# Attention and a bilinear GLU side by side on one core: other durations, leads and pauses in the planner that writes the order of work

## The chip, the cores and the metric

The kernel runs on one core of a Trainium2 chip. The metric is the device time of one execution in microseconds (us), the median of several runs. Before the change it is 2714.88 us (three runs, 2710.84 to 2721.91).

## The reference

What has to be computed, with S = 2048 rows, D = 576 columns, H = 32 heads of Dh = 18 and F = 4608 (the file writes the same with lambdas and einsum):

```python
xn  = layernorm(x)
# A: attention
q, k, v = heads(xn @ wqkv)
p   = softmax(q @ k.T * Dh ** -0.5)
s   = heads_joined(p @ v) @ wo
# B: bilinear GLU
h   = (xn @ w_gate) * (xn @ w_up)
g   = silu(h @ w_down)
out = x + s * g
```

All is float32. The kernel splits most operands into a high and a low part and multiplies three combinations of them, so one product of the reference is several matmuls here.

## The kernel before, in words

**Three stages.** A prologue normalises x, transposes it, makes q, k and v and spills q and k (`sqk`), v (`sv`) and the split columns of x (`sx`) to DRAM. The main stage computes attention and GLU together. The end stage multiplies the heads by `wo`, by the gate, and adds x.

**The main stage** has two streams of GLU work and two kinds of scores, and they share TensorE (PE) by rows of the array. Half 0 (rows 0 to 63) computes the up projection, half 1 (rows 64 to 127) the gate projection; matmuls of the two halves run at the same time if they stand next to each other in PE's queue. The GLU work comes in 72 units: 4 chunks of 512 rows of x by 18 pairs of 128 columns of F. In each unit both halves do two projections `n` of 27 matmuls with 512 columns (`gu_op`, L654), then the down projection of the unit before, 4 times 12 matmuls with 288 columns in each half (`down_op`, L682). `up_end` (L659) copies the up result on ACT; `gate_end` multiplies (L666, DVE), asks for the weights of projection n+2 (`g_get`, L183, DMA `wgu<-swg`), splits the product on ACT and POOL (L669, L670) and swaps halves by DMA (`hs<-hs`). `down_end` adds into `acc` (L710, DVE), and the last one of a unit asks for the next down weights (`d_get`, L216, DMA `wd<-swd`). In the first chunk the weights come raw and are split in small pieces on ACT and POOL (`piece`, L191/L192 and L222/L223) and stored for the later chunks.

**Scores.** For each head, 64 matmuls of the first kind (`a_item`, L558, usually half 0) give scores from which DVE takes maxima (L560). After the 64th, `max_fold` and `max_rows` (L566, L573, L574, L576) prepare the row maxima and write them into q by DMA. Then 64 matmuls of the second kind (`b_item`, L591, usually half 1) give scores that ACT exponentiates (L593). Each kind has two PSUM banks (`pa`, `pb`), the rest shares four (`pg`): a matmul may start in a bank only when the engine that reads it is done. When four groups of exponentials are there, a "visit" (`pv_group`, L602) multiplies them by v; it uses all 128 rows of the array, so both halves stop for it.

**The planner.** No engine chooses at run time: each runs its queue in order, and a wait at the head of PE's queue holds both halves. The order is written while the program is built. `order()` (L997) keeps a clock for each half (`clk`), a time at which DVE and ACT are free (`free`), a time at which each bank is free (`banks`), and a queue of DMAs at 0.24 MB per us (`moved`). At each step it takes the half whose clock is behind and gives it a score or the next matmul of its stream: a score when its bank is free and its goal (`a_goal`, `b_goal`, a pace over the whole stage) has passed, or when the stream may not go. `can_go` (L960) holds a stream back until its weights and inputs are believed to have landed (`loaded`, `there`, `downed`), and holds a gate projection until half 0 is `FIRST` us ahead. `lean` shifts the goals so that half 0 tends to be `SKEW` us ahead. `small` (L910) puts in the small chores: pieces of weights, and a list `later` that makes silu of a finished chunk and, after the first chunk, splits `wo` in five parts: `wo_load` (DMA into `wop`), `wo_high` (ACT, L766), `wo_low` (POOL, L770). Between two chores of `later` it lets 6 us of its own clock pass, or what `PAUSES` says.

The lines that the durations stand in, before:

```python
banks["a"][slot] = engine("DVE", clk[r] + 0.45, 0.70) + 0.06     # L872
clk[r] += 0.229                                                  # L873
rows_done[h] = engine("DVE", clk[r] + 0.45, 0.60) + ROWS         # L878
free[eng] = max(free[eng], start) + length - 0.09                # L837
clk[0] = clk[1] = now + 0.40                                     # L956, after a visit
```

Of the kernel before, what the change touches and what calls it, by code (L numbers as in the profile page):

```python
# [40 lines left out]
def kernel(  # L41
# [13 lines left out]
    H = 32  # L55
    DH = D // H
    assert S == 2048 and D == 576 and F % 256 == 0
    NT = S // 128
# [74 lines left out]
    chores, later = [], []  # L133
# [20 lines left out]
    units = [(c, q) for c in range(NCH) for q in range(NF2)]  # L154
# [51 lines left out]
    def d_get(n):  # L206
        if n >= len(units) - 1:
            return
        p = columns_of(n)
        if n and n % NF2 == 0:  # L210
            dw[n] = dw[n - 1]
            ddone.add(n)
            return
        w = dw[n] = d_tile()
        if n >= NF2:
            nc.sync.dma_start(w.bitcast(FT), swd[p])  # L216
            ddone.add(n)
            return
        raw = draw.pop(n)

        def piece(k):
            nc.scalar.activation(w[:, k, :, 0, :], raw[:, k], AF.Copy)  # L222
            nc.gpsimd.tensor_tensor(w[:, k, :, 1, :], raw[:, k], w[:, k, :, 0, :].bitcast(FT), op=OP.subtract)  # L223

        def end():
            ddone.add(n)
            nc.sync.dma_start(swd[p], w.bitcast(FT))
            d_load(n + 1)

        chores.extend([(piece, (k,)) for k in range(2)] + [(end, ())])  # L230

    R = 3 * DH

# [306 lines left out]
    with ExitStack() as mid:  # L540
# [236 lines left out]
        def wo_fetch():  # L777
# [2 lines left out]
            nc.sync.dma_start(wos[0].bitcast(FT), swo[:, 0:8, :])  # L780
            nc.sync.dma_start(wos[1].bitcast(FT), swo[:, 8:10, :])

        def stream(r):

            for u in range(len(units) + 1):
                for n in (2 * u, 2 * u + 1):
                    if u == len(units):
                        break
                    c, q = units[u]
                    box = []  # L790
                    for k in range(len(TERMS)):
                        def work(n=n, k=k, box=box, c=c, q=q):
                            if k == 0:
                                box.append(gu_start(r, n))
                            gu_op(r, n, box[0], k)
                            if q == NF2 - 1 and n % 2 and k % 3 == 2 and c < NCH - 1:
                                x_block(c + 1, k // 3, (64 * r,))
                                there["x", c + 1, k // 3, r] = moved(clk[r] + 0.5, 0.262)
                            if k == len(TERMS) - 1:
                                (gate_end if r else up_end)(n, box[0])  # L800
                                if r and n == 2 * len(units) - 1:
                                    wo_fetch()
                        end = (("DVE", 0.70) if r else ("ACT", 0.60)) if k == len(TERMS) - 1 else None
                        yield 0.229, k == 0, work, end, ("g", n, k)
                for s in range(4):
                    if not u:
                        break
                    box = []
                    for k in range(len(DTERMS)):
                        def work(s=s, k=k, box=box, u=u - 1):  # L810
                            if k == 0:
                                box.append(down_start(r, u))
                            down_op(r, u, s, box[0], k)
                            if k == len(DTERMS) - 1:
                                down_end(r, u, s, box[0])
                        end = ("DVE", 0.46) if k == len(DTERMS) - 1 else None
                        yield 0.131, k == 0, work, end, ("d", u - 1, 12 * s + k)

# [1 line left out]
        N = 64  # L822
        TOTAL = H * N
        LEAD, MOST = 24, 40
        PACE, SKEW, PULL, FIRST, ROWS = 1.01, 5.2, 3.0, 5.0, 6.0
        slots, gone = [0, 0], [0.0, 0.0]
        clk, free = [0.0, 0.0], {"DVE": 0.0, "ACT": 0.0}
        banks = {"a": [0.0] * 2, "b": [0.0] * 2, "g": [0.0] * 4}
        turn = {"a": 0, "b": 0}

        def next_free(tag):
            if tag == "g":
                return min(banks["g"])
            return banks[tag][turn[tag] % len(banks[tag])]

        def engine(eng, start, length):
            free[eng] = max(free[eng], start) + length - 0.09  # L837
            return free[eng] + 0.09

        def moved(start, size):  # L840

# [3 lines left out]
        due, jobs, rows_done = [], [], {}  # L845
        there, queue = {}, [0.0]
        na = nb = 0
        part = len(units) * (2 * 27 * 0.229 + 4 * 12 * 0.131) + (TOTAL + N + LEAD) * 0.229
        span = part + H * NT * (0.858 + 0.05)
        QUICK, LAST = 0.75, 0.75  # L850
        pace = (PACE * span - QUICK * N - LAST * (N + LEAD)) / (TOTAL - N)

# [8 lines left out]
        def a_next(r=0):  # L861
            nonlocal na
            h, i = divmod(na, N)
            if i == 0 and 2 <= h + 1 < H:
                stacks.append((0, h + 1))
            if i == 48 and (0, h + 1) in stacks:
                stacks.remove((0, h + 1))
                load_stack(0, h + 1)
            a_item(h, i, r)
            slot = turn["a"] % 2  # L870
            turn["a"] += 1
            banks["a"][slot] = engine("DVE", clk[r] + 0.45, 0.70) + 0.06  # L872
            clk[r] += 0.229  # L873
            na += 1
            if i == N - 1:
                max_fold(h)
                max_rows(h)
                rows_done[h] = engine("DVE", clk[r] + 0.45, 0.60) + ROWS  # L878

        def b_ready(r=1):  # L880
            h = nb // N
# [2 lines left out]
        def b_next(r=1):  # L884
            nonlocal nb
            h, i = divmod(nb, N)
            if i == 0 and h < H - 1:
                stacks.append((64, h + 1))
            if i == 48 and (64, h + 1) in stacks:
                stacks.remove((64, h + 1))  # L890
                load_stack(64, h + 1)
            if i == 16 and h % 2 == 0 and h // 2 + 1 < H // 2:
                load_v(h // 2 + 1)
            b_item(h, i, r)
            slot = turn["b"] % 2
            turn["b"] += 1
            end = engine("ACT", clk[r] + 0.45, 0.60)
            banks["b"][slot] = end + 0.06
            clk[r] += 0.229
            nb += 1  # L900
            if i % 4 == 3:
                due.append((h, i // 4, end + 0.1))

        KINDS = {"piece": ("ACT", 0.55), "first": ("ACT", 0.70), "second": ("DVE", 0.45), "inverse": ("DVE", 1.06),
                 "wo_high": ("ACT", 0.70)}
        PAUSES = {"wo_low": 16.0, "last": 16.0}

        quiet = [0.0]

        def small(now):  # L910

            q = chores or later
            if q is later and now < quiet[0]:
                return
            if q:
                eng, length = KINDS.get(q[0][0].__name__, ("POOL", 0.0))
                if eng == "POOL" or free[eng] <= now + 0.1 + (0.15 * (now - quiet[0]) if q is later else 0.0):
                    if eng != "POOL":
                        engine(eng, now, length)
                    if not chores:  # L920
                        quiet[0] = now + PAUSES.get(q[0][0].__name__, 6.0)
                    chore()

        def visit(now):

            now = max([now, *clk] + [j[0] for j in jobs])
            done = list(jobs)
            many = 0
            if due:
                now = max(now, next_free("g") - 0.1)  # L930
            now += 0.1
            for j in done:
                jobs.remove(j)
                j[1](j[2])
# [2 lines left out]
            for h, t, at in due:  # L937
                if at > now + 0.5 * many + 0.3 or h != due[0][0]:
                    break
                now += 0.864  # L940
                many += 1
            if many:
                k = banks["g"].index(next_free("g"))
                h = due[0][0]
                ts = [t for _, t, _ in due[:many]]
                pv_group(h, ts, k)
                end = engine("DVE", now + 0.2, 0.70) if ts[0] else engine("ACT", now + 0.2, 0.60)
                banks["g"][k] = end + 0.06
                if ts[-1] == NT - 1:
                    if h // 4 < H // 4 - 1:  # L950
                        finish(h)
# [1 line left out]
                    else:  # L953
                        jobs.append((end + 0.2, finish, h))
                del due[:many]
            clk[0] = clk[1] = now + 0.40  # L956

        upped, gated, downed = {}, {}, {}

# [21 lines left out]
        def late(goal, r=0):  # L981

            if goal + 4.0 <= clk[r]:
                return False
            fin = max(free["DVE"], clk[r] + 0.45) + 0.70
            for q in (0, 1):
                if heads[q] is None or heads[q][1]:
                    continue
# [8 lines left out]
        def order():  # L997
# [5 lines left out]
            while any(heads) or na < TOTAL or nb < TOTAL or due or jobs:  # L1003
# [28 lines left out]
                elif op is not None:  # L1032
# [3 lines left out]
                        slots[r] = banks["g"].index(next_free("g"))  # L1036
                        banks["g"][slots[r]] = 1e9
                    work()
                    clk[r] += length
                    gone[r] += length  # L1040
                    if end:
                        done = engine(end[0], clk[r] + 0.22, end[1])
                        banks["g"][slots[r]] = done + 0.06
                        if kind == "d":
                            if k == 47:
                                parts.setdefault(n, []).append(clk[r])
# [3 lines left out]
                            upped[n] = done  # L1050
                        else:
                            gated[n] = done
                            fin = engine("ACT", done + 0.1, 0.63)
                            loaded[n] = moved(done - 0.4, 1.18) if (n // 2 + 1) % NF2 else 0.0
                            lands = moved(fin + 1.3, 0.524)
                            if n % 2:
                                there["h", n // 2] = lands
                            if stacks:
# [118 lines left out]
```

## Time and profile before

| What | us |
|---|---|
| median of three runs | 2714.88 |
| the profiled execution | 2716.77 |
| its span, first to last instruction | 2715.0 |
| PE busy, of the span | 2659.6 |
| DVE busy | 1920.5 |
| ACT busy | 1483.5 |
| POOL busy | 451.2 |

A matmul on PE is recorded with its whole passage through the array, and matmuls of the two halves overlap; a busy PE may therefore still run one half alone. More is read from who waits at the head of PE's queue, and from the weight loads (PEld), which stand in the same queue. The mean granted clock of TensorE is 0.995.

### The profile page before, as it was taken

Reading aid. Unit: us, or ns where it says so; the run is one execution under the profiler, and the core shown is the slowest. Engines: PE = TensorE matmul, PEld = TensorE weight load, DVE = VectorE, ACT = ScalarE, POOL = GpSimd, SP = SyncE. Lnnn points to the kernel's source line nnn. Section 1 sums busy time; section 2 is a strip of 40 time slices with the busy share of each in tenths; the row PEclk is TensorE's granted clock in tenths of the full one; section 3 lists DMA queues with packets and bytes.
Section 4 is the critical chain, followed back from the end, with each engine's and each line's share of the span. In section 5 each row is a group of like instructions: output and inputs, shape, how many; then the busy total and the mean of one; then the engine's idle time right before and its main releaser. Section 6 shows DMA issues by size and latency. Waiting matters only on the chain.

```text
span 2715.0 us, 58960 instructions
## 1 busy us (share of the span) xinstructions
PE 2659.6 (98%) x24456; PEld 2125.0 (78%) x24456; DVE 1920.5 (71%) x3384; ACT 1483.5 (55%) x2726; POOL 451.2 (17%) x414
## 2 busy tenths in 40 slices
PE   7999999999999999989999999999999999999999
PEld 5898877777877787777868777877777787778779
DVE  7208777777777787767768777777777787767426
ACT  3222666666665565555645555555555565555552
POOL 2113333333311111111001111000000111000005
PEclk9999999999999999999999999999999999999999
DMA  6799887788795656666585555565676655564456
GB/s 210 221 292 253 242 224 204 204 237 216 217 224 153 182 167 174 185 171 192 148 193 153 169 164 171 161 183 161 173 180 164 184 160 171 166 162 138 149 168 206
DMA packets 212821, 508.63 MB, mean 187 GB/s; under 512 B 71112, under 2 KB 130888, under 8 KB 179016
## 3 DMA queue, kind: packets, MB, share of 16 engines
q1 hardware_dynamic: 209512, 493.64, 64.9%
q0 software_dynamic: 3040, 11.21, 1.1%
q8 instruction: 192, 3.15, 0.5%
q14 instruction: 77, 0.63, 0.1%
HBM read 314.05 MB, written 109.97 MB: 156 GB/s over the span
## 4 chain that ended last, share of the span: by engine, by line
PE 89%; DMA 4%; DVE 4%; issue 2%; POOL 1%; ACT 0%; SPq 0%; POOLq 0%; DVEq 0%; ACTq 0%
PE pg L654 31%; PE pg L602 16%; PE pg L682 13%; PE pa L558 11%; PE pb L591 8%; PE pg L1134 2%; PE pg L373 2%; PE pa L319 2%; PE pb L319 2%; DMA wgu<-swg 1%; DMA wd<-swd 1%; DVE mx L560 1%; DMA wop<-in_A_wo_dram 1%; DMA hs<-hs 0%; DVE us L666 0%
## 5 line engine op out<-in xcount | busy, mean ns | idle before, releaser
L654 PE MATMUL pg<-xc,wgu 64*128 64x512 f32 x7776 | 1667.5, 395 | 6.4 <-DMA wgu<-swg 4.5
L593 ACT ACTIVATE pt<-pb 128x512 f32<-128x512 f32 x2048 | 1173.8, 598 | 706.8 <-PE pb L591 546.3
L560 DVE TENSOR_REDUCE mx<-pa 128x1 f32<-128x512 f32 x2048 | 1354.0, 686 | 256.0 <-PE pb L591 117.7
L654 PEld LDWEIGHTS pg<-xc,wgu 64*128 64x128 f32 x7776 | 1152.7, 187 | 67.1 <-issue 8.4
L682 PE MATMUL pg<-wd,hs 64*128 64x288 f32 x6816 | 1048.6, 293 | 5.7 <-DMA wd<-swd 5.0
L682 PEld LDWEIGHTS pg<-wd,hs 64*128 64x128 f32 x6816 | 973.3, 186 | 32.5 <-issue 10.9
L558 PE MATMUL pa<-ks,qs 54*128 54x512 f32 x2048 | 820.3, 409 | 7.9 <-DVE mx L560 7.9
L591 PE MATMUL pb<-qs,ks 56*128 56x512 f32 x2048 | 816.2, 409 | 9.2 <-ACT pt L593 9.2
L558 PEld LDWEIGHTS pa<-ks,qs 54*128 54x128 f32 x2048 | 371.7, 185 | 140.1 <-issue 85.5
L670 POOL TENSOR_TENSOR hs<-us,hs 128x512 fp32r<-128x512 f32 x144 | 186.0, 1292 | 1764.1 <-ACT hs L669 1699.1
L602 PE MATMUL pg<-pt,vt 128*32 128x512 f32 x4096 | 468.1, 597 | 1.4 <-DVE us L666 1.4
L591 PEld LDWEIGHTS pb<-qs,ks 56*128 56x128 f32 x2048 | 368.0, 185 | 33.5 <-ACT pt L593 18.0
L602 PEld LDWEIGHTS pg<-pt,vt 128*32 128x32 f32 x4096 | 120.2, 110 | 265.5 <-issue 259.2
L608 DVE TENSOR_TENSOR oc<-oc,pg 128x512 f32<-128x512 f32 x98 | 67.5, 688 | 316.4 <-PE pg L602 313.8
L710 DVE TENSOR_TENSOR acc<-acc,pg 128x288 f32<-128x288 f32 x544 | 240.1, 446 | 49.5 <-PE pg L682 45.8
L669 ACT ACTIVATE hs<-us 128x512 fp32r<-128x512 f32 x144 | 91.2, 634 | 165.1 <-DVE us L666 165.1
L192 POOL TENSOR_TENSOR wgu<-wraw,wgu 128x384 fp32r<-128x384 f32 x108 | 108.0, 1015 | 148.5 <-ACT wgu L191 116.0
L666 DVE TENSOR_TENSOR us<-pg,us 128x512 f32<-128x512 f32 x144 | 98.5, 684 | 14.7 <-PE pg L654 7.0
L659 ACT ACTIVATE us<-pg 128x512 f32<-128x512 f32 x144 | 85.8, 596 | 21.7 <-PE pg L654 19.8
L606 ACT ACTIVATE oc<-pg 128x512 f32<-128x512 f32 x32 | 19.2, 600 | 104.2 <-PE pg L602 104.2
L223 POOL TENSOR_TENSOR wd<-draw,wd 128x576 fp32r<-128x576 f32 x36 | 51.0, 1430 | 82.6 <-ACT wd L222 64.7
L323 DVE TENSOR_TENSOR hl<-pb,hl 128x512 fp32r<-128x512 f32 x18 | 12.4, 691 | 72.5 <-ACT hl L322 72.4
(104 smaller groups left out, 1075.6 us busy)
## 6 DMA issues: line engine op xcount, KB each, us to landing
wgu<-swg SPq DMA_DIRECT2D x102, 1152.0 KB
hs<-hs SPq DMA_DIRECT2D x288, 256.0 KB
wd<-swd SPq DMA_DIRECT2D x50, 1152.0 KB
swg<-wgu SPq DMA_DIRECT2D x36, 1152.0 KB
qs<-sqk SPq DMA_DIRECT2D x192, 144.0 KB
ks<-sqk SPq DMA_DIRECT2D x192, 144.0 KB
swd<-wd SPq DMA_DIRECT2D x18, 1152.0 KB
sqk<-hl SPq DMA_DIRECT2D x32, 512.0 KB
```

The source lines that it names most:

```text
L192: nc.gpsimd.tensor_tensor(w[:, 9 + b:12 + b, :], raw[:, b:b + 3, :], w[:, b:b + 3, :].bitcast(FT), op=OP.subtract)
L319: nc.tensor.matmul(p, wq[b, a], xcs[c][:, e, :], start=n == 0, stop=n == len(PAIRS) - 1)
L558: nc.tensor.matmul(p, q[rows, t * 128:(t + 1) * 128], k[rows, c * 512:(c + 1) * 512], start=True, stop=True)
L560: nc.vector.tensor_reduce(mx[h][:, t, c:c + 1], p, axis=AX.X, op=OP.max)
L591: nc.tensor.matmul(p, k[rows, t * 128:(t + 1) * 128], q[rows, c * 512:(c + 1) * 512], start=True, stop=True)
L593: nc.scalar.activation(pt[t, c // 2][:, c % 2, :], p, AF.Exp, scale=scale)
L602: nc.tensor.matmul(p[32 * c:32 * c + 32, :], vt[h // 2][:, t, 6 * (h % 2):6 * (h % 2) + 32], pt[t, c // 2][:, c % 2, :], start=t == ts[0], ...
L654: nc.tensor.matmul(ps, gw[n][half[r], a, :], xg[i][half[r], e, :], start=k == 0, stop=k == len(TERMS) - 1)
L666: nc.vector.tensor_tensor(h32, ps, h32, op=OP.mult)
L670: nc.gpsimd.tensor_tensor(hj[:, 1, :], h32, hj[:, 0, :].bitcast(FT), op=OP.subtract)
L682: nc.tensor.matmul(ps[:, 0:HALF], hs[u][half[r], k, j, a, s * 128:(s + 1) * 128], dw[u][half[r], k, j, e, :], start=n == 0, stop=n == len( ...
L710: nc.vector.tensor_tensor(a, a, ps[:, 0:HALF], op=OP.add)
```

## The change

Only numbers of the planner and the way it keeps its clocks change; the instructions are the same ones, and so are their counts. The order in which they stand, and with it all waits, comes out anew.

- A matmul of 512 columns counts 0.2335 us instead of 0.229, one of 288 columns 0.1335 instead of 0.131. One clock `issued` for both halves is added: a matmul is not issued before the one ahead of it in the queue, and the first of each half after a visit takes 0.11 more.
- An engine's operation has an occupation, which sets when the next may start, and a tail until its result is there (`TAIL`): DVE's maximum 0.60 and 0.095 (before 0.61 and 0.09), ACT's exponential 0.495 and 0.115 (before 0.51 and 0.09). A bank comes free 0.03 after, not 0.06.
- POOL is followed too. Pieces of weights occupy ACT and then POOL; the swap of `hs` starts when POOL is done with it, by this account.
- The operations of `max_fold` and `max_rows` count 0.85 instead of 0.51. A visit's own overheads are changed (0.095 before it, 0.13 after it, 0.859 for each group).
- `SKEW` 5.2 becomes 3.0, `FIRST` 5.0 becomes 2.0; the pace of scores is worked out with the new durations.
- `PAUSES` has a new entry: 14 us after `wo_load`, where 6 held.
- The function `piece` of the down weights is renamed `dpiece`, so that it has durations of its own.

```diff
-        chores.extend([(piece, (k,)) for k in range(2)] + [(end, ())])
+        chores.extend([(dpiece, (k,)) for k in range(2)] + [(end, ())])
...
+        LONG, SHORT = 0.2335, 0.1335
...
-                        end = (("DVE", 0.70) if r else ("ACT", 0.60)) if k == len(TERMS) - 1 else None
-                        yield 0.229, k == 0, work, end, ("g", n, k)
+                        end = (("DVE", 0.60) if r else ("ACT", 0.50)) if k == len(TERMS) - 1 else None
+                        yield LONG, k == 0, work, end, ("g", n, k)
...
-                        end = ("DVE", 0.46) if k == len(DTERMS) - 1 else None
-                        yield 0.131, k == 0, work, end, ("d", u - 1, 12 * s + k)
+                        end = ("DVE", 0.365) if k == len(DTERMS) - 1 else None
+                        yield SHORT, k == 0, work, end, ("d", u - 1, 12 * s + k)
...
-        PACE, SKEW, PULL, FIRST, ROWS = 1.01, 5.2, 3.0, 5.0, 6.0
+        PACE, SKEW, PULL, FIRST, ROWS = 1.01, 3.0, 3.0, 2.0, 6.0
...
-        clk, free = [0.0, 0.0], {"DVE": 0.0, "ACT": 0.0}
+        clk, free = [0.0, 0.0], {"DVE": 0.0, "ACT": 0.0, "POOL": 0.0}
+        TAIL = {"DVE": 0.095, "ACT": 0.115, "POOL": 0.04}
+        issued, fresh = [0.0], [True, True]
...
-        def engine(eng, start, length):
-            free[eng] = max(free[eng], start) + length - 0.09
-            return free[eng] + 0.09
+        def engine(eng, start, taken):
+            free[eng] = max(free[eng], start) + taken
+            return free[eng] + TAIL[eng]
+
+        def issue(r, length):
+
+            at = issued[0] = max(clk[r], issued[0])
+            clk[r] = at + length + (0.11 if fresh[r] else 0.0)
+            fresh[r] = False
+            return at + (0.456 if length == LONG else 0.356)
...
-        part = len(units) * (2 * 27 * 0.229 + 4 * 12 * 0.131) + (TOTAL + N + LEAD) * 0.229
-        span = part + H * NT * (0.858 + 0.05)
+        part = len(units) * (2 * 27 * LONG + 4 * 12 * SHORT) + (TOTAL + N + LEAD) * LONG
+        span = part + H * NT * (0.859 - 0.01)
...
-            banks["a"][slot] = engine("DVE", clk[r] + 0.45, 0.70) + 0.06
-            clk[r] += 0.229
+            banks["a"][slot] = engine("DVE", issue(r, LONG), 0.60) + 0.03
...
-                rows_done[h] = engine("DVE", clk[r] + 0.45, 0.60) + ROWS
+                rows_done[h] = engine("DVE", 0.0, 0.85) + ROWS
...
-            end = engine("ACT", clk[r] + 0.45, 0.60)
-            banks["b"][slot] = end + 0.06
-            clk[r] += 0.229
+            end = engine("ACT", issue(r, LONG), 0.495)
+            banks["b"][slot] = end + 0.03
...
-                due.append((h, i // 4, end + 0.1))
+                due.append((h, i // 4, end + 0.03))
...
-        KINDS = {"piece": ("ACT", 0.55), "first": ("ACT", 0.70), "second": ("DVE", 0.45), "inverse": ("DVE", 1.06),
-                 "wo_high": ("ACT", 0.70)}
-        PAUSES = {"wo_low": 16.0, "last": 16.0}
+        KINDS = {"piece": (("ACT", 0.43), ("POOL", 1.02)), "dpiece": (("ACT", 0.59), ("POOL", 1.43)),
+                 "first": (("ACT", 0.59),), "second": (("DVE", 0.37),), "inverse": (("DVE", 0.96),),
+                 "last": (("POOL", 1.43),), "wo_high": (("ACT", 0.59),), "wo_low": (("POOL", 1.43),)}
+        PAUSES = {"wo_load": 14.0, "wo_low": 16.0, "last": 16.0}
...
+            now += 0.095
             if due:
-                now = max(now, next_free("g") - 0.1)
-            now += 0.1
+                now = max(now, next_free("g"))
...
-                now += 0.864
+                now += 0.859
...
-            clk[0] = clk[1] = now + 0.40
+            clk[0] = clk[1] = issued[0] = now + 0.13
+            fresh[:] = True, True
...
-                    clk[r] += length
+                    lands = issue(r, length)
                     gone[r] += length
                     if end:
-                        done = engine(end[0], clk[r] + 0.22, end[1])
-                        banks["g"][slots[r]] = done + 0.06
+                        done = engine(end[0], lands, end[1])
+                        banks["g"][slots[r]] = done + 0.03
...
-                            fin = engine("ACT", done + 0.1, 0.63)
+                            fin = engine("ACT", done + 0.05, 0.535)
+                            fin = engine("POOL", fin + 0.05, 1.29)
...
-                            lands = moved(fin + 1.3, 0.524)
+                            lands = moved(fin, 0.524)
```

More of the change, by code (lines that the diff above doesn't have):

```diff
@@ L219, in d_get, with dpiece @@
         raw = draw.pop(n)
-        def piece(k):
+        def dpiece(k):
             nc.scalar.activation(w[:, k, :, 0, :], raw[:, k], AF.Copy)
@@ L915, in small @@
             if q:
-                eng, length = KINDS.get(q[0][0].__name__, ("POOL", 0.0))
+                steps = KINDS.get(q[0][0].__name__, ())
+                eng = steps[0][0] if steps else "POOL"
                 if eng == "POOL" or free[eng] <= now + 0.1 + (0.15 * (now - quiet[0]) if q is later else 0.0):
-                    if eng != "POOL":
-                        engine(eng, now, length)
+                    at = now
+                    for eng, taken in steps:
+                        at = engine(eng, at + 0.05, taken)
                     if not chores:
@@ L946, in visit @@
                 pv_group(h, ts, k)
-                end = engine("DVE", now + 0.2, 0.70) if ts[0] else engine("ACT", now + 0.2, 0.60)
-                banks["g"][k] = end + 0.06
+                end = engine("DVE", now + 0.25, 0.60) if ts[0] else engine("ACT", now + 0.25, 0.495)
+                banks["g"][k] = end + 0.03
                 if ts[-1] == NT - 1:
@@ L984, in late @@
                 return False
-            fin = max(free["DVE"], clk[r] + 0.45) + 0.70
+            fin = max(free["DVE"], clk[r] + 0.45) + 0.60
             for q in (0, 1):
```

## The prediction

> **What bounds the kernel now.** I read the page first (shares, the chain that ended last), then the windows, then the waits of PE and of its weight loads, then the timeline around the longest waits. From the page:
>
> ```profile
> span 2715.0 us, 58960 instructions
> PE 2659.6 (98%) x24456; PEld 2125.0 (78%) x24456; DVE 1920.5 (71%) x3384; ACT 1483.5 (55%) x2726; POOL 451.2 (17%) x414
> ...
> PE 89%; DMA 4%; DVE 4%; issue 2%; POOL 1%; ACT 0%; SPq 0%; POOLq 0%; DVEq 0%; ACTq 0%
> ```
>
> PE sets the end; no other engine is over 71%. But 98% says little here, because PE counts as busy while one half runs alone. The main stage by itself (span, PE, weight loads, DVE, ACT, POOL, granted clock, DMA share):
>
> ```profile
> 208.00:2640.00 2432.00, 2401.53 (x22897) 1891.69 (x22896) 1797.70 (x3144) 1401.31 (x2526) 371.75 (x319) 1.00 0.66 182
> ```
>
> The change touches the main stage alone, 2432 us; the other 283 us of the span stay. In it the number of matmuls is fixed, so what can be won is time in which a half has nothing or the head of the queue waits. The waits of PE, then of the weight loads:
>
> ```profile
> PE pb L591 <- ACT pt L593: 9.2, 4, 7.3
> PE pa L558 <- DVE mx L560: 7.9, 11, 1.8
> PE pg L682 <- DMA wd<-swd: 5.0, 4, 2.8
> PE pg L654 <- DMA wgu<-swg: 4.5, 4, 2.8
> PE pg L654 <- DMA xc<-sx: 0.7, 2, 0.5
> ```
>
> ```profile
> PEld pa L558 <- DVE mx L560: 33.4, 104, 2.2
> PEld pb L591 <- ACT pt L593: 18.0, 37, 7.7
> PEld pg L682 <- DMA wd<-swd: 6.7, 4, 3.3
> PEld pg L654 <- DMA wgu<-swg: 5.4, 5, 3.2
> PEld pg L654 <- DMA xc<-sx: 1.6, 2, 0.9
> ```
>
> The first fence is time in which the array stood still, 9.2 + 7.9 + 5.0 + 4.5 + 0.7 = 27.3 us. The second counts the same stalls and many short ones that a running matmul partly hides, 65.1 us. Those are the bounds of what waiting costs. To them comes the clock:
>
> ```profile
> 1187.00:1212.00 25.00, 17.68 (x144) 14.62 (x144) 13.00 (x21) 11.68 (x21) 3.74 (x4) 0.86 0.69 176
> 1397.00:1420.00 23.00, 19.49 (x161) 14.80 (x157) 13.94 (x23) 10.66 (x19) 1.27 (x1) 0.93 0.97 223
> 2373.00:2392.00 19.00, 16.21 (x144) 13.54 (x144) 11.90 (x21) 10.27 (x19) 0.00 (x0) 0.91 0.80 173
> ```
>
> In each window with a long wait the granted clock falls, to 0.86, 0.93 and 0.91. A stall is paid twice: while it lasts, and while the clock is low behind it.
>
> **The change part by part.** Counts of instructions are equal in both kernels, and so are the 131 visits, nearly all of four groups. What differs is where things stand, and that I take from the two orders set side by side; distances in them I turn into us with the rows below.
>
> *A. The pause after `wo_load`.*
>
> ```profile
> 1187.51 0.60 ACT L606 ACTIVATE oc<-pg 128x512 f32<-128x512 f32 x1 [3.15 <-PE pg L602]
> 1195.55 0.68 ACT L766 ACTIVATE wop<-wop 128x576 fp32r<-128x576 f32 x1 [7.44 <-DMA wop<-in_A_wo_dram]
> ```
>
> The fourth `wo_high` stood in ACT's queue 7.44 us before its data came; the exponentials (L593) behind it waited, the `pb` banks stayed full, and PE stopped (the 7.3 above). A later `wo_high` cost some 0.7 in the same way (of the 9.2). In the old order `wo_high` comes 6 to 8 us of PE work after `wo_load`, in the new one 14 to 16. The 8 us more cover 7.44 by little, if the DMA lands as late again. Removed: 7.3 + 0.7, and of the clock 25 x 0.14 = 3.5 us, of which about half falls on time in which PE ran: **-9.5**. What is late next: nothing, since a later `wo_high` delays only the list of chores; five pauses of 8 us more make 40 us, and `wo` is needed only when the main stage ends at 2640.
>
> *B. Weights and inputs that land late.* The DMA rows give 10.2 us by PE, 13.7 by the loads. With the clock behind two of them (23 x 0.07 + 19 x 0.09 = 3.3) that is at most 17. Less lead (`SKEW`, `FIRST`) means that half 0 reaches new weights later after half 1 let the old ones go. In the orders, from the issue of `wgu<-swg` to half 0's first use there are in the tightest tenth 9.4 us of PE work before and 17.9 after (least 8.7 and 11.0); for `wd<-swd` at least 7.6 before and 12.8 after. Half 1's distances stay at about 20. So each of these waits, 3.3 us at the longest, has its length covered twice, apart from the x blocks at a change of chunk, which gain nothing. **-11** (bounds 0, if the queue itself is late, and -17).
>
> *C. The end of the main stage.*
>
> ```profile
> 2618.97 0.50 PE L591 MATMUL pb<-qs,ks 56*128 56x512 f32 x2
> 2619.31 1.08 PE L682 MATMUL pg<-wd,hs 64*128 64x288 f32 x7
> ...
> 2627.00 1.81 PE L602 MATMUL pg<-pt,vt 128*32 128x512 f32 x8
> ```
>
> By the old order half 0 has one matmul in these 8.0 us and half 1 has 39: half 0 ran out early. In the new order the last stretches are even (9.81 us of work in both, then 3.84 and 5.47). Adding up for all stretches between visits the work of the fuller half gives 1857.9 us before and 1851.8 after: **-6**.
>
> *D. The start.* One half alone, then both:
>
> ```profile
> 222.42 0.62 PE L654 MATMUL pg<-xc,wgu 64*128 64x512 f32 x2
> 222.89 0.39 PE L558 MATMUL pa<-ks,qs 54*128 54x512 f32 x1
> ...
> 1126.47 0.93 PE pg L654 x8
> ```
>
> Alone, three matmuls (L654 twice, L558 once) take 0.70 us, 0.233 each (222.42 to 222.89, and on at that pace); together, eight take 0.93, also 0.23 in each half. Before the first visit the old order lets half 1 run 31 and then 12 matmuls alone, the new one 16 and 13, a difference of 14 x 0.233 = 3.3 us; half 1 also starts its first gate 3 us earlier (`FIRST`). **-3** (bounds 0 and -6).
>
> *E. Maxima and banks.*
>
> ```profile
> 482.24 2.80 POOL L223 TENSOR_TENSOR wd<-draw,wd 128x576 fp32r<-128x576 f32 x2 [1.83 <-ACT wd L222]
> 482.87 0.83 DVE L573 TENSOR_SCALAR mm<-m 128x16 fp32r<-128x16 f32 x1
> 483.74 1.33 DVE L574 SCALAR_TENSOR_TENSOR mm<-m,mm 128x16 fp32r<-128x16 f32 x1
> 485.94 0.49 PE L558 MATMUL pa<-ks,qs 54*128 54x512 f32 x1 [1.77 <-DVE mx L560]
> ...
> L573 DVE TENSOR_SCALAR mm<-m x32: 174/175/1186, 259.0 to 2543.5; 128x16 fp32r<-128x16 f32 x32
> ```
>
> The long waits for DVE stand behind `max_rows`. Its steps take 0.175 each as a rule (the median in the last row) and 0.83 and 1.33 while POOL works. The planner's 0.85 for the whole fits the undisturbed case; nothing keeps POOL away from these steps, so the long waits mostly stay. In a sentence apart: the Trainium skill, GPSIMD Engine Reference, Key points, says that POOL shares its SBUF interfaces with VectorE and contends with its instructions in a 2-port mode or with two SBUF inputs; by that rule, which speaks against the change and with which these rows agree, none of the 1.77 goes.
>
> Then the banks:
>
> ```profile
> 2388.30 0.39 PE L558 MATMUL pa<-ks,qs 54*128 54x512 f32 x1
> 2388.73 0.69 DVE L560 TENSOR_REDUCE mx<-pa 128x1 f32<-128x512 f32 x1 [1.18 <-PE pb L591]
> ...
> 279.11 1.29 DVE L560 TENSOR_REDUCE mx<-pa 128x1 f32<-128x512 f32 x2
> ...
> L710 DVE TENSOR_TENSOR acc<-acc,pg 128x288 f32<-128x288 f32 x544 | 240.1, 446 | 49.5 <-PE pg L682 45.8 <-PE pa L558 0.7 <-PE pb L591 0.4
> ```
>
> From matmul to maximum 0.43, the maximum 0.69, then some 0.05 until PE goes on: a bank is back after 1.17 us at best, and two maxima in a row take 1.29 - 0.69 = 0.60 each. The new planner's sums (0.456 + 0.60 + 0.095 + 0.03 = 1.18; 0.60) are these values; the old ones were 1.21 and 0.61. In the old order no score of the first kind comes back to its bank within 1.25 us but two; in the new one 269 of 2048 come at 1.167. Each misses by a hundredth of a us at best; with an `acc` (0.446) between, by a few tenths. Against that, halves' clocks that are right to a hundredth should take away many of the 104 short waits. Bounds: -15 (half of the 33.4, nothing new) to +27 (269 at 0.1). I take **-2**, near what the rows of the floor give.
>
> *Hidden at no cost:* the renamed `dpiece` and the POOL clock alter only when chores stand in ACT's queue, which is 55% busy; without that cover a piece costs its 0.5 us. The visits' constants move no instruction but through the clocks.
>
> **Sum**, against the profiled execution of 2716.8 us (span 2715.0): -9.5 - 11 - 6 - 3 - 2 = -31.5, so 2685. It lies 1.9 above the median of the runs; against the median **2684** is my number, rounded.
>
> One rule of the pages on the clock, which the sum does not need: the Trainium skill, TensorE: Matmul & The Clock Gate, section "What's actually happening", says that PE falls to half clock after at least one idle window of about 3.4 us. By it only A would bring clock back, and B would be 3.3 us smaller, giving 2687. The trace differs: the windows at 1397 and 2373 show 0.93 and 0.91 with stalls of 2.8 us at most.
>
> **The rivals.**
>
> *R1, the queue is what is late.* The DMA share is 0.97 in the window at 1397. If transfers land late because the queue is full, an earlier place in the order issues into the same jam: B gives -3, `wop` lands later than 14 us too and A gives -4, C and D stay with half. Then 2716.8 - 3 - 4 - 4.5 = 2705, against the median 2703. For it: that share, and the 7.44 that the new pause covers by little. Against it: the windows at 1187 and 2373 show 0.69 and 0.80.
>
> *R2, the tight banks.* The 269 returns at 1.167 are planned without slack; whenever DVE has an `acc` or a product in hand, the score waits at the head of the queue and holds both halves. At 0.18 us each (less than half of an `acc`) they cost 48 us and the result is 2685 + 48 = 2733, slower. It decides from (31.5 + 13.6) / 269 = 0.17 on. For it: DVE is the busiest of the others, and one disturbed `max_rows` (1.77) shows what a late bank does. Against it: the planner puts every `acc` on DVE's clock at its measured 0.36 of occupation, so a random half `acc` is not to be expected.
>
> *R3, more than I take:* all upper ends of A, B, D, E: -10 - 17 - 6 - 6 - 15, which is 2663 and below.
>
> **How the numbers follow.** About 0.5%, 13.6 us, is what a measurement of this kernel can tell from no change. The forecast (some 2660 to 2701) gets 0.68, R3 beyond that 0.05, R1 with all that ends between 2701 and 2728 0.14, R2 0.13. So faster 0.73, same 0.14, slower 0.13. The range 2658 to 2714 leaves out R2 and the outer part of R1, together under 2 in 10.
>
> **What the profile after would show.** A: no idle of several us before L766 on ACT, the longest wait of L591 under 1.5. B: `wgu<-swg` and `wd<-swd` gone from PE's waits or under 3 us together; the windows of the clock at 1.00 except at the chunks' changes. C: both halves in the last 20 us, L591 not alone. D: the first visit some 3 us earlier. E: PE's and the loads' wait for L560 at about 30 us and the same long ones beside POOL; R2 would show there, with 80 us or more. I am wrong if the waits of PE shrink as said and the span does not, since then one half idles where no wait is shown.

## The result and the profile after

The changed kernel takes 2689.61 us (median of four runs, 2687.2 to 2691.63), the kernel before 2717.05 in the same comparison: ratio 0.990, 95% interval 0.9877 to 0.9923, or 27 us less (21 to 33). The forecast was 2684.

The page of the changed kernel, its shares and its chain:

```profile
span 2685.4 us, 59017 instructions
...
PE 2649.1 (99%) x24456; PEld 2053.7 (76%) x24456; DVE 1917.8 (71%) x3384; ACT 1476.2 (55%) x2726; POOL 451.2 (17%) x414
...
PE 93%; DVE 3%; DMA 2%; issue 1%; ACT 1%; POOL 1%; SPq 0%; POOLq 0%; ACTq 0%; DVEq 0%
```

The page counts 57 instructions more than before; those of PE, DVE, ACT and POOL are as many as they were, and the work of DVE, ACT and POOL is the same to a few us; PE's share of the chain rises from 89% to 93%, the DMAs' falls from 4% to 2%. Two stretches, the main stage and the end stage (span, PE, weight loads, DVE, ACT, POOL, clock, DMA share):

```profile
208.00:2610.00 2402.00, 2391.27 (x22897) 1820.51 (x22897) 1796.42 (x3144) 1394.03 (x2526) 371.65 (x319) 1.00 0.67 184
2610.00:2686.00 76.00, 68.45 (x528) 67.98 (x528) 48.03 (x86) 18.55 (x64) 40.23 (x52) 0.97 0.62 209
```

The 22897 matmuls that took 2432 us now take 2402. All of the gain, 30 us by the two profiles, lies in the main stage. Who PE waits for there (sum in us, count, longest):

```profile
PE pg L654 <- DMA xc<-sx: 3.8, 5, 1.3
PE pg L682 <- DVE acc L710: 3.3, 6, 1.6
...
PE pb L591 <- ACT pt L593: 1.8, 4, 1.0
```

In place of 27.3 us these rows add up to 8.9. `wgu<-swg` and `wd<-swd` are gone, L591's long wait too. What grew is a wait of the weight loads, from 33.4 us over 104 times:

```profile
PEld pa L558 <- DVE mx L560: 55.2, 250, 0.5
...
PEld pb L591 <- ACT pt L593: 10.8, 43, 1.3
PEld pg L654 <- DMA xc<-sx: 7.0, 8, 1.7
```

250 short waits for a maximum, none over 0.5 us. The forecast had put this at about 30 us.

The clock gains too. In the traces the granted clock is 0.50 for stretches of 3.41 us. The main stage before has seven of them (around 282, 487, 1194 twice in a row, 1415, 2385 and 2627), the changed kernel two (275 and 1385; the first is not at a change of chunk, where alone the prediction expected any). What one costs can be seen in the kernel before, where the visit at 2627 falls into a stretch and the one ahead of it does not:

```profile
2627.20:2630.60 3.40, 3.40 (x20) 0.87 (x16) 0.00 (x0) 0.50 (x2) 0.00 (x0) 0.50 0.01 1
```

```profile
2615.40 3.64 PE L602 MATMUL pg<-pt,vt 128*32 128x512 f32 x32
...
2627.00 5.34 PE L602 MATMUL pg<-pt,vt 128*32 128x512 f32 x32
```

The same 32 matmuls take 1.7 us more. Five stretches fewer are then worth up to 8.5 us, an estimate, since not all of them fall wholly on work.

### The profile page after: what moved, and what is told of

Read it like the earlier page. It is cut to its first block, busy times and chain, and to the rows that moved or that the text cites. A ratio compares the mean times of both kernels' runs of the same rounds, so it can differ in the third digit from the quotient of the medians.

```text
span 2685.4 us, 59017 instructions
## 1 busy us (share of the span) xinstructions
PE 2649.1 (99%) x24456; PEld 2053.7 (76%) x24456; DVE 1917.8 (71%) x3384; ACT 1476.2 (55%) x2726; POOL 451.2 (17%) x414
## 4 chain that ended last, share of the span: by engine, by line
PE 93%; DVE 3%; DMA 2%; issue 1%; ACT 1%; POOL 1%; SPq 0%; POOLq 0%; ACTq 0%; DVEq 0%
PE pg L654 32%; PE pg L602 17%; PE pg L682 15%; PE pa L558 12%; PE pb L591 8%; PE pg L1148 2%; PE pg L373 2%; PE pa L319 2%; PE pb L319 2%; DMA xc<-sx 1%; DVE mx L560 1%; DVE xn L282 0%; DMA draw<-in_B_w_down_dram 0%; POOL wgu L192 0%; DVE st L271 0%
## 5 line engine op out<-in xcount | busy, mean ns | idle before, releaser
L593 ACT ACTIVATE pt<-pb 128x512 f32<-128x512 f32 x2048 | 1167.1, 597 | 686.6 <-PE pb L591 541.5
L560 DVE TENSOR_REDUCE mx<-pa 128x1 f32<-128x512 f32 x2048 | 1356.8, 685 | 247.4 <-PE pb L591 114.0
L654 PE MATMUL pg<-xc,wgu 64*128 64x512 f32 x7776 | 1387.8, 394 | 4.4 <-DMA xc<-sx 3.8
L654 PEld LDWEIGHTS pg<-xc,wgu 64*128 64x128 f32 x7776 | 993.3, 186 | 88.4 <-DMA xc<-sx 7.0
L558 PE MATMUL pa<-ks,qs 54*128 54x512 f32 x2048 | 830.4, 414 | 0.1
L591 PE MATMUL pb<-qs,ks 56*128 56x512 f32 x2048 | 820.0, 412 | 1.8 <-ACT pt L593 1.8
L682 PE MATMUL pg<-wd,hs 64*128 64x288 f32 x6816 | 775.3, 294 | 3.3 <-DVE acc L710 3.3
L682 PEld LDWEIGHTS pg<-wd,hs 64*128 64x128 f32 x6816 | 731.8, 185 | 28.6 <-issue 13.4
L558 PEld LDWEIGHTS pa<-ks,qs 54*128 54x128 f32 x2048 | 370.7, 184 | 168.0 <-issue 83.8
L591 PEld LDWEIGHTS pb<-qs,ks 56*128 56x128 f32 x2048 | 366.5, 184 | 27.4 <-ACT pt L593 10.8
L710 DVE TENSOR_TENSOR acc<-acc,pg 128x288 f32<-128x288 f32 x544 | 233.4, 445 | 27.1 <-PE pg L682 25.0
L666 DVE TENSOR_TENSOR us<-pg,us 128x512 f32<-128x512 f32 x144 | 98.2, 682 | 23.2 <-PE pg L654 22.8
```

The source lines that it names most:

```text
L558: nc.tensor.matmul(p, q[rows, t * 128:(t + 1) * 128], k[rows, c * 512:(c + 1) * 512], start=True, stop=True)
L560: nc.vector.tensor_reduce(mx[h][:, t, c:c + 1], p, axis=AX.X, op=OP.max)
L591: nc.tensor.matmul(p, k[rows, t * 128:(t + 1) * 128], q[rows, c * 512:(c + 1) * 512], start=True, stop=True)
L593: nc.scalar.activation(pt[t, c // 2][:, c % 2, :], p, AF.Exp, scale=scale)
L654: nc.tensor.matmul(ps, gw[n][half[r], a, :], xg[i][half[r], e, :], start=k == 0, stop=k == len(TERMS) - 1)
L666: nc.vector.tensor_tensor(h32, ps, h32, op=OP.mult)
```

## The experiments

**The theories.** Theory 1 is that of the prediction: each part takes away its own waits (the pause the wait for `wop`, the shorter leads those for weights, the clocks the uneven end), and the parts add. Theory 2: faithful clocks carry the gain, and the rest is chance of a new order. A second question came with the profile: what do the 250 short waits cost? Each kernel has its ratio to the kernel before from five rounds.

**The pause alone**, on the kernel before:

```diff
-        PAUSES = {"wo_low": 16.0, "last": 16.0}
+        PAUSES = {"wo_load": 14.0, "wo_low": 16.0, "last": 16.0}
```

> The kernel before with the 14 us pause after wo_load as its only change. Theory 1 (the gains of the parts stand beside each other, as in the prediction): the wait of L591 for ACT at 1196 goes with its slow clock, 7 to 10 us less than before, and nothing else moves. Theory 2 (the clocks of the planner carry the gain, the rest is chance): within 4 us of before, since the wop transfer is late in the jam whatever the pause.

2708.08 against 2715.51, ratio 0.9971 (0.9961 to 0.9980): 7.4 us less. Of the waits of PE, that of L591 went from 9.2 to

```profile
PE pb L591 <- ACT pt L593: 1.5, 2, 1.3
```

while those for `wgu` and `wd` together grew from 9.5 to 12.1 us. Theory 1 holds for the size of this part; that nothing else would move does not hold.

**The leads alone**, on the kernel before:

```diff
-        PACE, SKEW, PULL, FIRST, ROWS = 1.01, 5.2, 3.0, 5.0, 6.0
+        PACE, SKEW, PULL, FIRST, ROWS = 1.01, 3.0, 3.0, 2.0, 6.0
```

> The kernel before with SKEW 3.0 and FIRST 2.0 as its only change. Theory 1: the waits for wgu and wd and the slow clock behind them go, the start gains some us: 10 to 16 us less than before; the wo_high wait stays. In this order the tightest tenth of the wgu loads has 17.4 us of PE work, as in the changed kernel, and the uneven end stays (fuller halves 1858.0 us). Theory 2: under 5 us less.

2706.69 against 2715.51, ratio 0.9965 (0.9952 to 0.9978): 8.8 us less, under the 10 to 16 of theory 1. The waits of PE in this kernel say why:

```profile
PE pg L682 <- DMA wd<-swd: 9.5, 1, 9.5
PE pg L602 <- ACT pt L593: 5.1, 1, 5.1
PE pb L591 <- ACT pt L593: 4.8, 5, 3.6
```

The wait for `wgu` is down to 0.8 us, near what was said; but one single load of down weights at a change of chunk stops PE for 9.5 us, longer than all waits for `wd` before, and behind `wo_high` ACT is late twice: PE waits 9.9 us for L593 in all, where it was 9.2 before.

**The clocks alone**: the changed kernel with `SKEW` 5.2, `FIRST` 5.0 and no entry for `wo_load`.

> The changed kernel with the old SKEW 5.2 and FIRST 5.0 and without the pause: the planner's clocks, occupations and pace alone. Theory 1: only the even end and the tight banks act: fuller halves 1854.8 us, 3 us less than before, 204 scores under 1.18 us from their bank's last use, which cost 5 to 8 us; so between 6 us less and 5 us more than before, with waits for wgu and wd as in the kernel before. Theory 2: 20 us less or better, nearly all of the change.

2704.84 against 2715.51, ratio 0.9961 (0.9945 to 0.9976): 10.7 us less, outside both expectations. It is two fifths of the gain, not nearly all, and more than an even end gives. Most of it can be read in the rows: PE's waits for maxima fall from 7.9 to 4.0, those for `wd` from 5.0 to 0.3, those for `wgu` from 4.5 to 3.9, and two stretches of half clock go; against that more scores are close. The wait for `wop` is still there (PE waits 10.0 us for L593, 9.2 before), in the ACT timeline of this kernel:

```profile
1230.51 0.68 ACT L766 ACTIVATE wop<-wop 128x576 fp32r<-128x576 f32 x1 [10.92 <-DMA wop<-in_A_wo_dram]
```

**Leads and pause together**, on the kernel before, with the old clocks.

> The kernel before with SKEW 3.0, FIRST 2.0 and the 14 us pause, and with the old clocks. If the parts add (7.4 for the pause and 8.8 for the leads by their runs): 16 us less than before. If they hide each other (both free the same stretches of the DMA queue): 9 to 11 us less.

2691.17 against 2716.41, ratio 0.9911 (0.9896 to 0.9925): 25.2 us less, where the sum is 16.2. They neither add nor hide each other; together they give more.

**Without the pause, and without the leads**, each taken out of the changed kernel.

> The changed kernel without the 14 us pause after wo_load. If the pause is worth inside the change what it was worth alone (7.4): 2695 to 2699, with a wait of some us of L591 for ACT behind wo_high. Rival (with shorter leads the DMA queue is freer and wop lands in time without it): within 3 us of the changed kernel.

> The changed kernel with the old SKEW 5.2 and FIRST 5.0. The runs so far leave two accounts. Alone on the old clocks the leads gave 8.8, and with the pause 25.2 together, 17.8 more than the pause alone. If they are worth the larger sum: 2704 to 2710, with waits for wgu and wd of 5 to 10 us. If the new clocks already avoid these waits: 2693 to 2698, near clocks alone plus the pause (2717 - 10.7 - 7.4).

2689.30 without the pause, ratio 0.9907 (0.9893 to 0.9920); 2691.01 with the old leads, ratio 0.9914 (0.9900 to 0.9927). Both are within 2 us of the changed kernel's 2689.61. In the first the rival stands, but not for its reason: `wop` does come late, four times, up to 4.88 us,

```profile
1140.44 0.68 ACT L766 ACTIVATE wop<-wop 128x576 fp32r<-128x576 f32 x1 [4.88 <-DMA wop<-in_A_wo_dram]
```

yet PE waits for L593 only 3.6 us in all. In the second the waits for weights are back,

```profile
PE pg L654 <- DMA wgu<-swg: 4.8, 4, 2.4
...
PE pg L682 <- DMA wd<-swd: 1.3, 2, 0.7
```

and the weight loads wait less for maxima (38.7 us, 164 times), because this order has fewer close scores (204 were counted in it without the pause, the changed kernel has 269): a gain against a loss. That the two balance is read from these rows, not shown by a run of its own.

All eight combinations, in us against the kernel before of the same comparison:

| | old clocks | new clocks |
|---|---|---|
| old leads, no pause | 0 | -10.7 |
| pause | -7.4 | -23.2 |
| shorter leads | -8.8 | -24.9 |
| both | -25.2 | -27.4 |

One part gives 7 to 11, any two 23 to 25, the third 2 to 4 more, too little to be told from nothing when the whole change lies between 21 and 33. The three parts alone add up to 26.9, almost the 27.4 of all together; since any two give more than their sum, that is chance.

The rows show in part why two give more. What the pause removes is larger once the order is another. On the kernel before it takes PE's waits for L593 from 9.2 to 1.5, while those for weights grow. With the leads in place it takes them from 9.9 to 1.2 (the load of `wd` still costs 8.2 there), and the stretches of half clock from eight to four. With the new clocks it takes them from 10.0 to 1.8, and the stretches from five to two.

**Close scores.** The changed planner counts a bank free 0.03 us after the maximum's result. One number is changed in it:

```diff
-            banks["a"][slot] = engine("DVE", issue(r, LONG), 0.60) + 0.03
+            banks["a"][slot] = engine("DVE", issue(r, LONG), 0.60) + 0.09
```

> The changed kernel with 0.09 us instead of 0.03 from the end of a maximum until its bank counts as free: 24 scores under 1.18 us from their bank's last use, where the changed kernel has 269. Theory 1 (tight banks cost what the weight loads' wait for L560 grew by): the wait of 55.2 us over 250 falls to about 30 and the time is 5 to 10 us less than that of the changed kernel. Rival: a short wait at the bank only takes the place of a wait at the next one, the score could not have been issued earlier anyway: within 3 us of the changed kernel, while the wait shrinks all the same.

2669.56, ratio 0.9830 (0.9812 to 0.9848): 20 us less than the changed kernel, twice what theory 1 gave. Then only 15 ns more slack than the changed kernel has (0.045), and much more (0.20):

> The changed kernel with 0.045 us instead of 0.03 from a maximum's end until its bank is free: 15 ns more, and 34 scores at 1.167 us from their bank's last use where the changed kernel has 269. Theory (it is the number of scores whose weight load finds the bank not yet free, each a matmul of 0.49 in place of 0.39, that costs the 20 us): as good as the run with 0.09, 17 to 23 us less than the changed kernel. Rival (slack itself pays, in proportion): a quarter of it, some 5 us less.

> The changed kernel with 0.20 instead of 0.03: no score comes back to its bank under 1.18 us and 6 under 1.3 (with 0.09: 24 and 93). If every weight load that waits costs, the 93 still cost some: 3 to 6 us less than the run with 0.09. Rival: the scores come later than their pace and the order around them gets worse: within 3 us of it, or more.

With 0.045, 2675.58, ratio 0.9854 (0.9836 to 0.9871): 14 us less for 15 ns of slack. That is nearer to the theory than to its rival, though short of its 17. With 0.20, 2660.35, ratio 0.9797 (0.9781 to 0.9813): 9 us less than with 0.09, more than either expected. A small part of these gains may be the clock: the main stage has one stretch of half clock with 0.09 and none with 0.045 and 0.20, where the changed kernel has two, an estimated 1.7 to 3.4 us. And the reverse, close scores put into the kernel before:

```diff
-            banks["a"][slot] = engine("DVE", clk[r] + 0.45, 0.70) + 0.06
+            banks["a"][slot] = engine("DVE", clk[r] + 0.45, 0.70) + 0.0
```

> The kernel before with 0.00 instead of 0.06 from a maximum's end until its bank is free, which puts 214 scores under 1.18 us from their bank's last use where it has none. Theory of the weight loads: 214 x 0.075 = 16 us more than before, and more scores of 0.49. Rival (in the old order the halves are off their plan by more than that anyway): within 4 us of before.

2725.94 against 2716.41, ratio 1.0037 (1.0024 to 1.0049): 9.5 us more, over half of what the theory gave and clear of the rival. It is a net figure: in this order other waits of PE are shorter than before (`wgu` 1.3 against 4.5, `wd` 3.2 against 5.0, L591 6.7 against 9.2), so that the close scores cost more than 9.5. The waits of the weight loads for L560, in the order 0.20, 0.09, 0.045, changed kernel, kernel before with close scores: 2.2, 10.2, 20.4, 55.2 and 65.5 us (33.4 in the kernel before). The first and the last of them as the views give them:

```profile
PEld pa L558 <- DVE mx L560: 2.2, 9, 0.5
```

```profile
PEld pa L558 <- DVE mx L560: 65.5, 209, 1.9
```

How so short a wait costs so much stands in the timeline. The changed kernel, a close score (start, duration):

```profile
476.36 0.18 PEld L558 LDWEIGHTS pa<-ks,qs 54*128 54x128 f32 x1 [0.28 <-DVE mx L560]
476.36 0.49 PE L558 MATMUL pa<-ks,qs 54*128 54x512 f32 x1
476.36 0.18 PEld L591 LDWEIGHTS pb<-qs,ks 56*128 56x128 f32 x1
476.36 0.50 PE L591 MATMUL pb<-qs,ks 56*128 56x512 f32 x1
...
476.69 0.63 PE L654 MATMUL pg<-xc,wgu 64*128 64x512 f32 x4
```

The kernel with 0.20, a score with room:

```profile
476.14 0.18 PEld L558 LDWEIGHTS pa<-ks,qs 54*128 54x128 f32 x1
476.25 1.28 DVE L560 TENSOR_REDUCE mx<-pa 128x1 f32<-128x512 f32 x2
476.37 0.39 PE L558 MATMUL pa<-ks,qs 54*128 54x512 f32 x1
```

With room the weights are loaded 0.23 us ahead, while the matmul before runs, and the score takes 0.39. The close score's wait stands at its weight load: the load starts when the bank is free, and with it the matmul, which then takes 0.49. The score of the other half, whose load is next in the queue, takes 0.50 as well, and the next L654 comes 0.33 after, not 0.23. So a close score is not 0.01 us late, as its start says, but costs both halves 0.1. This is the rule and not one example: of the scores of the first kind that the changed kernel runs at full clock in the main stage, 356 start together with their load (within 0.015 us). They take 0.495 us in the mean, and the next matmul that does not run beside them starts 0.335 later (median). The 892 whose load started 0.20 to 0.26 ahead take 0.392. Scores that start with their load number 127 with 0.20, 194 with 0.09, 212 with 0.045, 261 in the kernel before and 379 in it with close scores. The Trainium skill, TensorE: Matmul & The Clock Gate, section "Step-by-step: what each phase is for", says that PE pulls weight loads ahead of running matmuls; the trace agrees where nothing is waited for (0.23 us ahead), and shows 0 where the bank is not free. The mean of L558 (the last number but one, in ns) follows through the runs, in the changed kernel and with 0.20:

```profile
L558 PE MATMUL pa<-ks,qs 54*128 54x512 f32 x2048 | 830.4, 414 | 0.1
```

```profile
L558 PE MATMUL pa<-ks,qs 54*128 54x512 f32 x2048 | 803.4, 400 | 0.1
```

From 414 to 400 ns, times 2048 scores, is 28.7 us; the time fell by 29.3. With 0.045 the mean is 407, which gives 14.3 against 14.0 measured, and with 0.09 it is 406, 16.4 against 20.

**Both kinds of scores**: the second kind's bank gets room too.

```diff
-            banks["a"][slot] = engine("DVE", issue(r, LONG), 0.60) + 0.03
+            banks["a"][slot] = engine("DVE", issue(r, LONG), 0.60) + 0.20
...
-            banks["b"][slot] = end + 0.03
+            banks["b"][slot] = end + 0.16
```

> The changed kernel with 0.20 for the first kind's banks and 0.16 instead of 0.03 for the second kind's: 97 scores of the second kind at under 1.18 us from their bank's last use, where the run with 0.20 alone has 298. If a weight load that waits for ACT costs what one that waits for DVE does: 200 x 0.05 = 10 us less than the run with 0.20. Rival (the second kind's engine, ACT, is 55% busy and frees its banks in time; an exponential ends in 0.60, a maximum in 0.69): within 3 us of it.

> As the run before it, with 0.20 for both kinds and a pace of scores of 1.00 in place of 1.01, which evens the end (fuller halves 1853.0 us; with 1.01 it would be 1858.0): 60 scores of the second kind under 1.18 us. By the account of the weight loads: 0 to 5 us less than the run with 0.16. Rival (scores that come later collide more often with visits): more than that run.

2652.68 with 0.16, ratio 0.9771 (0.9757 to 0.9784): 7.7 us less than with 0.20 for the first kind alone, so ACT's banks cost the same way, if a little less than expected. With 0.20 and the pace 1.00 it is 2653.72, ratio 0.9776 (0.9763 to 0.9790), no different. But its main stage is shorter: from 208 us on it has run 22896 matmuls by 2570, the run with 0.16 has 22892 by 2575. The end stage loses that again in one wait for a DMA, which the run with 0.16 does not have:

```profile
PE pb L1125 <- DMA oin<-so: 5.2, 1, 5.2
```

The kernel with 0.20 and 0.16 beats both kernels: 62 us less than before, 37 less than the change. The page of it:

```profile
span 2650.9 us, 59017 instructions
...
PE 94%; DVE 3%; DMA 1%; issue 0%; ACT 0%; SPq 0%; POOL 0%; POOLq 0%; ACTq 0%; DVEq 0%
```

## Why the prediction was right, and where it was not

The sum, -31.5, came out at -27.4 (-33 to -21). (From the median of the kernel before the sum gives 2683.4; the 2684 is that, rounded up.) Its terms did not come out so evenly.

- **A, the pause, -9.5:** measured alone 7.4; the mechanism was right, the size near. Inside the changed kernel nothing of it can be told from noise (2689.30 without it; 2.5 by the ratios). The step that failed is the silent one that the terms add. In the changed kernel without the pause `wop` is late as well, but a visit of 3.64 us falls into its longest wait on ACT (4.88 us, from 1135.56 on), and PE stands for 1.05 behind it:

```profile
1135.40 3.64 PE L602 MATMUL pg<-pt,vt 128*32 128x512 f32 x32
...
1141.66 0.50 PE L591 MATMUL pb<-qs,ks 56*128 56x512 f32 x1 [1.05 <-ACT pt L593]
```

- **B, the weights, -11, and D, the start, -3:** the waits for `wgu` and `wd` went as forecast, those for the x blocks did not gain, as said, and grew from 0.7 to 3.8. The first visit, before and after:

```profile
304.03 0.64 PE L602 MATMUL pg<-pt,vt 128*32 128x512 f32 x4
```

```profile
300.46 0.64 PE L602 MATMUL pg<-pt,vt 128*32 128x512 f32 x4
```

  is 3.6 us earlier, as D had it. But alone the leads gave 8.8 for 14, since one load of `wd` took 9.5 us and the late `wop` 9.9, and inside the change they are worth 1.4 (4.2 by the ratios), which noise can hide.
- **C, the end, -6:** no run has it by itself. Half 1 is alone for the last 2.3 us (from 2596.35 on) instead of most of 8, so L591 does still stand alone, but briefly:

```profile
2596.19 0.30 PE L682 MATMUL pg<-wd,hs 64*128 64x288 f32 x1
2596.35 0.49 PE L591 MATMUL pb<-qs,ks 56*128 56x512 f32 x1
...
2598.64 1.92 PE L602 MATMUL pg<-pt,vt 128*32 128x512 f32 x16
```

  The new clocks alone gave 10.7 with this in them. The stretch of half clock at 2627, behind the uneven end before, has no counterpart here; if it belongs to that end, its 1.7 us come on top of the 6.
- **E, maxima and banks, -2:** the term of the sum that was mis-sized, on both of its sides. "I take -2, near what the rows of the floor give": the floor of 1.17 us was right (the closest returns in the changed kernel lie there), but I priced the lateness of the matmul and not its weight load. Taking close scores out of the changed kernel gave 14 us (0.045) to 20 (0.09), or 0.06 to 0.08 for each of the 235 and 245 that went, inside the stated bound of +27 and far from what the floor gave. On the other side PE's own waits for L560, which the prediction let mostly stay, fell from 7.9 to 0.1. Against the kernel before, which has 261 scores that start with their load already, the changed one has 356; at 0.1 us each that is 9.5 more, and with the 7.8 that went E is some +2, an estimate. That this is near -2 is luck. Rival R2 named the same scores, with another mechanism (an `acc` in DVE's hand, waited for at the head of the queue) and too high a price: the head waits 0.1 us in all, and a close score costs less than the 0.17 from which R2 would have decided. The disturbed steps behind the long waits are still there,

```profile
1132.23 1.18 DVE L573 TENSOR_SCALAR mm<-m 128x16 fp32r<-128x16 f32 x1
1133.44 1.32 DVE L574 SCALAR_TENSOR_TENSOR mm<-m,mm 128x16 fp32r<-128x16 f32 x1
```

  beside POOL's work as before; but what waits behind these two is an `acc` (L682 for L710, 1.6 us of 3.3 in all), not a score.
- **R1, the queue is what is late:** it did not come. PE's waits for weights vanished although the DMA share of the main stage is 0.67, as before 0.66. In the two runs with the short leads on the old clocks something like it did come, once in each: a late load of `wd` stopped PE for 9.5 and 8.2 us.

So the nearness of the whole is in part luck. The parts alone add up to almost the gain of the whole, though no two of them add. E came out near its -2 with both of its sides off. And the clocks alone gave 10.7, where C and E stood for -8, partly through waits that the sum had put under B (`wd` 5.0 to 0.3). What two parts give beyond their sum is shown for the pause, by the rows above; how much of the rest belongs to which part stays open: each new order places the late DMAs anew, so that a run shows where it lost but not which part did it.

## What to carry to other kernels

A planner that is right about durations to a hundredth of a us can take away its own safety: give a buffer's return as much room as the consumer's preparation needs (here the 0.2 us of a weight load), not only until the buffer is free. Price a wait at the instruction that carries it, with all that it would have done ahead, and look at the durations of the waiting instruction as well as at its waits. Gains that each remove a stall need not add: measure parts alone and left out before their sum is believed.

## What the runs showed of the hardware

- A score (a matmul of 512 columns) that starts together with its weight load took 0.49 us instead of 0.39, and the next L654 started 0.33 after it instead of 0.23; the other half's score beside it took 0.50 (the rows at 476.36).
- The granted clock falls to 0.50, for stretches of 3.41 us, after stalls that are short. In the changed kernel the window around the change of the second chunk, where PE waits four times, 1.3 us at the longest, has one stretch and shows 0.91 in the mean:

```profile
1375.00:1395.00 20.00, 17.30 (x139) 12.94 (x139) 14.32 (x25) 9.69 (x17) 0.00 (x0) 0.91 1.05 216
```

  The Trainium skill, TensorE: Matmul & The Clock Gate, section "What's actually happening", asks for an idle window of about 3.4 us; the measurement differs.
- `max_rows`' two small DVE steps of 0.175 us take 1.18 and 1.32 while POOL works. Both end within 0.03 us of the end of the POOL instruction that was running when they started:

```profile
1132.09 1.29 POOL L670 TENSOR_TENSOR hs<-us,hs 128x512 fp32r<-128x512 f32 x1 [7.70 <-ACT hs L669]
1133.34 1.40 POOL L770 TENSOR_TENSOR wop<-wop 128x576 fp32r<-128x576 f32 x1
```
